# Finding a capacity threshold in four halving rounds, with the gating and picking work laid out in thinner pieces

## The chip, the cores and the metric

The kernel runs on one core of a Trainium2 chip. The metric is the device time of one launch in microseconds, taken as the median of the runs. The core's engines work in parallel, each on its own queue of instructions in program order: TensorE (PE in the profile), VectorE (DVE), ScalarE (ACT), GpSimd (POOL) and SyncE (SP, here only a DMA queue). An instruction that waits holds back everything behind it on its engine.

## The reference, cut to what matters

Eight batches of 2,496 tokens of 256 channels go through a filter in the frequency domain. The 19,968 tokens that come out are gated to eight experts, and each expert keeps the 80 tokens with the largest gate; all other output rows are zero.

```python
X = np.fft.rfft(x, axis=1)                          # x: (8, 2496, 256)
y = np.fft.irfft(X * (filt_r + 1j * filt_i)[None], n=2496, axis=1)
x = y.reshape(8 * 2496, 256)
logits = x @ w_gate                                  # (19968, 8)
expert_idx = np.argmax(logits, axis=1)
probs = softmax(logits); gate_w = probs[arange, expert_idx]
for e in range(8):
    tok_idx = np.where(expert_idx == e)[0]
    if len(tok_idx) > 80:
        tok_idx = tok_idx[np.argpartition(-gate_w[tok_idx], 80)[:80]]
    h = np.maximum(x[tok_idx] @ w1[e], 0.0)          # w1[e]: (256, 1024)
    out[tok_idx] = gate_w[tok_idx, None] * (h @ w2[e])
```

## The kernel before

The length 2,496 is split as 39 x 64, so that the two transforms are matrix products. The last transform is not done for all tokens: the logits come from the half-transformed data, the kept tokens are found, and only rows that may be kept are transformed to the end.

**First phase.** `step(k)` runs for k = 0 to 81, ten steps for each batch. `stage2` of a step is eight matmuls into `pb` (TensorE, L405), one multiplication by the filter into `p` (VectorE, L410) and two combinations into `yt` (GpSimd, L416 and L418). `turn` of the step two back is eight matmuls into `py` (L428), which ScalarE copies out (L450 and L453). `put(k, at, f)` hangs other work on a step: at 0 ahead of `stage2`, at 1 between `stage2` and `turn`, at 2 behind `turn`. The numbers in `put` are written by hand, and they set the order on every engine's queue. Hung on the steps 42 to 72 are:

- `logits_e` (40 matmuls L469, a sum on VectorE) and `logits` of a batch: transposes into `ps` (L481), two copies into `s` on ScalarE (L483), matmuls into `pl` (L490), two copies into `lg` on ScalarE (L495).
- `gating` of one or two batches in six parts: part 0 is a maximum and a difference `sh` on VectorE, then `ex` and `no` on ScalarE (L520, L523); part 1 a DMA; parts 2 and 3 turn `ex` into the `key` on VectorE (L529 to L536, where `key` has the tile of `ex`); part 4 transposes the keys on TensorE into `pk` (L549), copied by ScalarE into `kt`; part 5 finds the eight largest keys of each partition row of a batch, the candidates `cand`.
- `pick`, a generator: each `next` runs it to its next `yield`, one piece. Every partition row belongs to one expert, and 16 rows to each. Its pieces are: the 16 largest candidates of each row, sorted, in `row`, and laid out in `spread`; a matmul that puts all 16 x 16 = 256 of an expert on each of its rows (`pall`, L592) and the count for every one of the 16 sorted values of a row of how many of the 256 are above it; the threshold `tau`, the `kept` candidates and their number `cnt`; offsets through TensorE (`poff`, L632); the compaction into 16 codes (`ccode`); their fields (`fi`, `bval`); two one-hot blocks `bplc` (L687); the list of row indices `idxb` through TensorE (L694). The first pick takes the batches 0 to 4 with a larger share kept, and gives the lists for the gathers; the final pick takes all batches.

The count is the Sign function on ScalarE with its accumulator, one ACTIVATE over 128 x 256 for each of the 16 values:

```python
for k in range(KR):                                   # KR = 16
    nc.scalar.activation(out=pall[:, 256:256 + 16 * KR], in_=pall[:, 0:16 * KR],
                         func=AF.Sign, scale=-1.0, bias=row[:, k:k + 1],
                         accum_out=bal[:, k:k + 1])
    if k % 4 == 3:
        yield
```

`fetch(t)` is a gather on GpSimd's queue (L885): 128 rows of 10 KB, by the list of one batch. The first one stands on step 72, with GpSimd's `yt` operations behind it.

**Second phase.** 41 slots. Slot i transposes four blocks of gathered rows into `pw` (`turn_rows`, L935), which ScalarE copies into `wt` (L936); then `rows_out(i - 1)` multiplies the `wt` of the slot before with kept spectra (eight matmuls into `po`, L948). Five slots make a batch. `aside` gives each slot the work that follows it: logits and gating of the batches 5 to 7, the pieces of the final pick (`last_pick`), loads of spectra and weights. `turn_rows` of a batch's last slot issues the gather of the batch after next.

**Last.** If a count of violations is not zero, a fallback selects again in a slow way; then the two matrix products of the experts run on the gathered rows. One violation is a row that keeps 16 candidates or more (`viol`).

## Time and profile before

| | us |
|---|---|
| median of 3 runs | 510.12 (507.42 to 512.67) |
| profiled execution, its own time | 504.71 |
| its span, first to last instruction | 502.9 |
| TensorE busy in the span | 442.3 (88%) |
| VectorE, ScalarE, GpSimd busy | 174.8, 180.2, 154.0 |

The profiled execution is one more run of the same kernel, 5.4 us under the median of the others, and 1.8 us of its time lie outside the span. A row of the trace gives the start and the duration of an instruction or of a run of equal ones, and in brackets how long its engine had been idle and what it waited for. The steps 0 to 81 lie ahead of about 302 us in the span, the slots of the second phase from about 306 to 397 us.

### The profile page before, as it was taken

What the parts mean: (1) busy time and instruction counts of PE and PEld (TensorE: products, weight loads), DVE (VectorE), ACT (ScalarE), POOL (GpSimd) and SP (SyncE); (2) the same over time, 40 slices, a digit from 0 to 9 for tenths busy, and PEclk for the clock granted to TensorE, in tenths of its full rate; (3) what the DMA queues carried; (4) which work ended last, traced back from release to release, by engine and by line L of the source; (5) the groups of instructions that cost most, each with busy time, mean ns of one, the idle gap of its engine ahead of it and who ended that gap; (6) DMA issues with size and microseconds to landing.
All of it is one profiled execution on the core that took longest, in us unless ns stands there. A gap on an engine that the chain in (4) does not pass through costs nothing. (4 is left out here: it accounts for less than half of the span.)

```text
span 502.9 us, 7871 instructions
## 1 busy us (share of the span) xinstructions
PE 442.3 (88%) x2907; PEld 375.7 (75%) x2907; DVE 174.8 (35%) x344; ACT 180.2 (36%) x452; POOL 154.0 (31%) x218
## 2 busy tenths in 40 slices
PE   4989988889999999879987989985998992799995
PEld 4888766567877878769987988664887882788883
DVE  2555332234434334572858741241430000001100
ACT  1224344453454353751473333538222220001111
POOL 4032212225445443431663780000225003200111
PEclk9999999999999999995997998998999997569999
DMA  6869999998999994696899655359498866929500
GB/s 220 230 197 271 329 354 407 405 361 271 339 287 341 396 398 162 215 314 212 269 371 382 247 186 233 120 202 339 163 376 327 283 224 196 347 72 334 189 15 13
DMA packets 69532, 133.21 MB, mean 265 GB/s; under 512 B 5428, under 2 KB 51892, under 8 KB 67824
## 3 DMA queue, kind: packets, MB, share of 16 engines
q1 hardware_dynamic: 58982, 92.05, 54.6%
q10 hardware_dynamic: 8074, 28.27, 14.2%
q0 software_dynamic: 2432, 12.33, 7.2%
q8 instruction: 25, 0.41, 0.3%
q14 instruction: 19, 0.16, 0.1%
HBM read 81.56 MB, written 51.07 MB: 264 GB/s over the span
## 5 line engine op out<-in xcount | busy, mean ns | idle before, releaser
L410 DVE TENSOR_TENSOR p<-pb,ft 128x1024 f32<-128x1024 f32 x80 | 97.8, 1222 | 96.6 <-PE pb L405 91.0
L416 POOL TENSOR_TENSOR yt<-p 128x256 f32<-128x256 f32 x80 | 60.0, 750 | 176.0 <-PE py L428 114.6
L428 PEld LDWEIGHTS py<-gi,yt 128*128 128x128 f32 x640 | 83.7, 194 | 18.8 <-issue 11.7
L405 PE MATMUL pb<-d_t,t 128*128 128x128 f32 x640 | 88.4, 282 | 7.1 <-ACT t L351 5.8
L428 PE MATMUL py<-gi,yt 128*128 128x136 f32 x640 | 89.9, 284 | 4.6 <-POOL yt L418 4.0
L405 PEld LDWEIGHTS pb<-d_t,t 128*128 128x128 f32 x640 | 80.5, 197 | 10.1 <-ACT t L351 6.5
L349 PE MATMUL pa<-x,wf_t 128*128 128x512 f32 x128 | 60.0, 595 | 0.5 <-ACT t L351 0.4
L418 POOL TENSOR_TENSOR yt<-p 128x256 f32<-128x256 f32 x80 | 58.9, 736 | 0.0
L351 ACT COPY t<-pa 128x512 f32<-128x512 f32 x64 | 36.2, 588 | 51.6 <-PE pa L349 25.7
L948 PE MATMUL po<-yb,wt 128*128 128x256 f32 x160 | 39.9, 394 | 7.7 <-ACT wt L936 7.7
L948 PE MATMUL po<-yk,wt 128*128 128x256 f32 x160 | 37.9, 381 | 2.8 <-ACT wt L936 2.8
L936 ACT COPY wt<-pw 128x512 f32<-128x512 f32 x40 | 23.2, 584 | 47.2 <-PE pw L935 41.8
L948 PEld LDWEIGHTS po<-yb,wt 128*128 128x128 f32 x160 | 29.9, 197 | 11.9 <-ACT wt L936 8.4
L1067 PEld LDWEIGHTS ph<-xs,w 128*128 128x128 f32 x256 | 36.1, 227 | 1.1 <-DVE xs L1063 0.5
L450 ACT COPY ysp<-py 128x512 f32<-128x512 f32 x40 | 23.3, 584 | 37.2 <-PE py L428 24.3
L1067 PE MATMUL ph<-xs,w 128*128 128x80 f32 x256 | 36.1, 311 | 0.3 <-DVE xs L1063 0.3
L349 PEld LDWEIGHTS pa<-x,wf_t 128*128 128x128 f32 x128 | 22.1, 191 | 19.0 <-issue 15.5
L450 ACT COPY yk<-py 128x512 f32<-128x512 f32 x40 | 23.4, 585 | 30.1 <-PE py L428 27.3
L948 PEld LDWEIGHTS po<-yk,wt 128*128 128x128 f32 x160 | 29.1, 191 | 6.4 <-ACT wt L936 3.3
L370 PE MATMUL pn<-wn_t,x 117*128 117x120 f32 x176 | 23.8, 297 | 9.6 <-DMA x<-in_x_dram 8.0
L1081 PE MATMUL po<-w,hT 128*80 128x256 f32 x128 | 31.9, 400 | 0.0
L370 PEld LDWEIGHTS pn<-wn_t,x 117*128 117x128 f32 x176 | 22.8, 212 | 10.1 <-DMA x<-in_x_dram 7.2
(165 smaller groups left out, 384.5 us busy)
## 6 DMA issues: line engine op xcount, KB each, us to landing
out_dram<-zero_t SPq DMA_DIRECT2D x26, 768.0 KB
x<-in_x_dram SPq DMA_DIRECT2D x32, 512.0 KB
d<-t ACTq DMA_DIRECT2D x32, 512.0 KB
w<-in_moe_w_dram SPq DMA_DIRECT2D x16, 1024.0 KB
t<-d SPq DMA_DIRECT2D x30, 512.0 KB
yf<-ysp ACTq DMA_DIRECT2D x20, 512.0 KB
yb<-yf SPq DMA_DIRECT2D x4, 2560.0 KB
x<-in_x_dram SPq DMA_DIRECT2D x25, 156.0 KB
```

The lines of the kernel that those rows point to most:

```text
L349: nc.tensor.matmul(out=ps, lhsT=wf_t, rhs=xt[:, 2 * i:2 * i + 2, :], start=True, stop=True)
L351: nc.scalar.copy(out=t1[:, 2 * i:2 * i + 2, :], in_=ps)
L370: nc.tensor.matmul(out=ps[:, j].rearrange("p h s r -> p (h s r)"), lhsT=xt[0:NP1, j, 128 * cb:128 * cb + 128], rhs=wn_t, start=True, stop= ...
L405: nc.tensor.matmul(out=ps[:, i, cb], rhs=d_t[:, s, :], start=True, stop=True, lhsT=st["t2", b, s // SG][:, s % SG, 128 * cb:128 * cb + 128])
L410: nc.vector.tensor_tensor(out=pt, in0=ps[:].rearrange("p s c r q -> p (s c) r q").unsqueeze(1).to_broadcast(shape), in1=ft[:, u].unsqueeze ...
L416: nc.gpsimd.tensor_tensor(out=yt[:, :, 0, :], in0=pt[:, 0, :, 0, :], in1=pt[:, 1, :, 1, :], op=AL.subtract)
L418: nc.gpsimd.tensor_tensor(out=yt[:, :, 1, :], in0=pt[:, 0, :, 1, :], in1=pt[:, 1, :, 0, :], op=AL.add)
L428: nc.tensor.matmul(out=ps[:, i, 136 * cb:136 * cb + 136], rhs=gi[:, cb, :], lhsT=yt[:, 2 * i + cb].rearrange("p r q -> p (r q)"), start=Tr ...
L450: nc.scalar.copy(out=ys[:, m:m + 2, :].rearrange("p i (k c) -> p i k c", k=NDB), in_=ps[:, :, 0:288].rearrange("p i (k c) -> p i k c", k=N ...
L948: nc.tensor.matmul(po, lhsT=wts[i][:, m, :], rhs=yk[b][g][:, m, :], start=(s == 0), stop=(s == NS - 1))
L1067: nc.tensor.matmul(ph[:, fc // 4, fc % 4, 0:cap], lhsT=w1s[e][:, k, 128 * fc:128 * fc + 128], rhs=xs[:, k, :], start=(k == 0), stop=(k == ...
L1081: nc.tensor.matmul(po[0:cap, :], lhsT=hT[:, fc, :], rhs=w2s[e][:, fc, :], start=(fc == 0), stop=(fc == NFC - 1))
```

## The change

The 256 values on a row are the same as before, and so is the matmul. The 16 counts become four rounds of a halving search over the 16 sorted values: a round counts for one value (the eighth, then by the outcome so far one four, two, one places on), and VectorE works out the next place `at` and picks that value from `row` by a one-hot product with an accumulator. `low`, from which the threshold comes, is then made from the place found. A row may now keep at most 14, not 15, before it counts as a violation, since the search doesn't tell the last place from the end.

The places of the work are changed too. `logits` keep theirs but for batch 4, one step later. `gating(0)`'s six parts stand on the steps 47, 47, 48, 49, 51, 52 (before 47, 48, 48, 48, 49, 50), `gating(2)`'s on 53, 53, 54, 55, 57, 58 (before 50, 51, 51, 51, 52, 53), `gating(4)`'s on 59, 59, 60, 60, 62, 63 (before 54, 55, 55, 56, 57, 58). The pieces of the first pick stand on 64 to 69, 71 to 74 and 76, ahead of `stage2` (before: 59 to 70, behind `turn`), and the first gather on step 76 (before 72). In the second phase the logits and gating of the batches 5 to 7 come up to one slot earlier, the pieces of the final pick one to a slot from slot 9 to 25 (before 8 to 23, three in slot 10), and the gather of batch 5 moves from the transposes of slot 19 to the side work of slot 20.

```diff
--- before.py
+++ after.py
@@ -588,16 +588,37 @@
                 in1=thot[:].unsqueeze(2).to_broadcast([128, 16, KR]), op=AL.mult)
             yield
 
+
             pall = fps.tile([128, 512], F32, name=f"pall_{nm}", tag="f")
             nc.tensor.matmul(pall[:, 0:16 * KR], lhsT=same_f[:],
                              rhs=spread[:].rearrange("p t k -> p (t k)"), start=True, stop=True)
-            bal = tl([128, KR], F32, "bal")
-            for k in range(KR):
+            at = None
+            for i, h in enumerate((8, 4, 2, 1)):
+                if i == 0:
+                    val = row[:, h - 1:h]
+                else:
+                    vrow = tl([128, KR], F32, "vrow")
+                    vt = tl([128, 1], F32, "val")
+                    nc.vector.scalar_tensor_tensor(
+                        out=vrow[:], in0=iota[:, 0:KR], scalar=at[:, 0:1], in1=row[:],
+                        op0=AL.is_equal, op1=AL.mult, accum_out=vt[:, 0:1])
+                    val = vt[:, 0:1]
+                bal = tl([128, 1], F32, "bal")
                 nc.scalar.activation(out=pall[:, 256:256 + 16 * KR], in_=pall[:, 0:16 * KR],
-                                     func=AF.Sign, scale=-1.0, bias=row[:, k:k + 1],
-                                     accum_out=bal[:, k:k + 1])
-                if k % 4 == 3:
-                    yield
+                                     func=AF.Sign, scale=-1.0, bias=val, accum_out=bal[:, 0:1])
+                yield
+
+                nxt = tl([128, 1], F32, f"at{i}")
+                nc.vector.tensor_scalar(out=nxt[:], in0=bal[:], scalar1=16.0 * KR - 2.0 * kc,
+                                        scalar2=float(h), op0=AL.is_ge, op1=AL.mult)
+                if i == 0:
+                    nc.vector.tensor_scalar(out=nxt[:], in0=nxt[:], scalar1=h / 2.0 - 1.0,
+                                            scalar2=None, op0=AL.add)
+                else:
+                    nc.vector.scalar_tensor_tensor(
+                        out=nxt[:], in0=nxt[:], scalar=-h / 2.0 if h > 1 else 0.0, in1=at[:],
+                        op0=AL.add, op1=AL.add)
+                at = nxt
 
 
             if final:
@@ -609,8 +630,8 @@
             nc.vector.tensor_scalar(out=some[:], in0=row[:], scalar1=1e-30, scalar2=None,
                                     op0=AL.is_ge, op1=AL.add, accum_out=npos[:, 0:1])
             low = tl([128, KR], F32, "low")
-            nc.vector.tensor_scalar(out=low[:], in0=bal[:], scalar1=16.0 * KR - 2.0 * kc,
-                                    scalar2=4.0, op0=AL.is_lt, op1=AL.mult)
+            nc.vector.tensor_scalar(out=low[:], in0=iota[:, 0:KR], scalar1=at[:, 0:1],
+                                    scalar2=4.0, op0=AL.is_ge, op1=AL.mult)
             nc.vector.tensor_tensor(out=low[:], in0=low[:], in1=row[:], op=AL.add)
             tau = tl([128, 1], F32, "tau")
             nc.vector.tensor_reduce(out=tau[:], in_=low[:], axis=AX.X, op=AL.min)
@@ -702,7 +723,7 @@
                                     scalar2=None, op0=AL.max)
 
             v0 = 4 * nm
-            nc.vector.tensor_scalar(out=viol[:, v0:v0 + 1], in0=rcnt[:], scalar1=float(KR),
+            nc.vector.tensor_scalar(out=viol[:, v0:v0 + 1], in0=rcnt[:], scalar1=float(KR - 1),
                                     scalar2=None, op0=AL.is_ge)
             vb = tl([128, B], F32, "vb")
             nc.vector.tensor_scalar(out=vb[:, 0:n_b], in0=poff[:, 1, nb0:nb], scalar1=128.0,
@@ -858,22 +879,21 @@
         k = NU * 4 + LATE
         for i in range(3):
             put(k + i, 2, part(logits_e, 0, i))
-        for b in range(4):
-            k = NU * 4 + LATE + 3 + b + b // 2
-            put(k, 1, part(logits, b, 0, 0, b % 2))
-            put(k, 2, part(logits, b, 0, 1, b % 2))
-            if b % 2:
-                for i, at in enumerate((0, 1, 1, 1, 2, 3)):
-                    put(k + 1 + at, 2, part(gating, b - 1, i))
+        for b, at in ((0, 3), (1, 4), (2, 6), (3, 7)):
+            put(k + at, 1, part(logits, b, 0, 0, b % 2))
+            put(k + at, 2, part(logits, b, 0, 1, b % 2))
+        for b0, at0 in ((0, 5), (2, 11)):
+            for i, at in enumerate((0, 0, 1, 2, 4, 5)):
+                put(k + at0 + at, 2, part(gating, b0, i))
 
         k = NU * NA + LATE
         put(k, 2, part(logits_e, 4, 0))
-        put(k + 1, 1, part(logits, 4, 4, 0, 0))
-        put(k + 1, 2, part(logits, 4, 4, 1, 0))
-        for i, at in enumerate((2, 3, 3, 4, 5, 6)):
+        put(k + 2, 1, part(logits, 4, 4, 0, 0))
+        put(k + 2, 2, part(logits, 4, 4, 1, 0))
+        for i, at in enumerate((7, 7, 8, 8, 10, 11)):
             put(k + at, 2, part(gating, 4, i))
-        for at in (7, 8, 9, 10, 11, 12, 13, 14, 15, 16, 17, 18):
-            put(k + at, 2, more_pick)
+        for at in (12, 13, 14, 15, 16, 17, 19, 20, 21, 22, 24):
+            put(k + at, 0, more_pick)
         for i in range(14):
             put(NU * 4 + 4 + 2 * i, 2, part(put_zeros, 1))
 
@@ -892,8 +912,8 @@
             pools["m"] = fctx.enter_context(tc.tile_pool(
                 name="mp", bufs=1, side="right", reuse_waits="tile"))
 
-        put(NU * (B - 1) + LATE - 1, 2, make_room)
-        put(NU * (B - 1) + LATE, 2, part(fetch, 0))
+        put(k + 24, 1, make_room)
+        put(k + 24, 1, part(fetch, 0))
 
         ahead(0)
         chunk()
@@ -934,7 +954,7 @@
                 s = SG * g + m
                 nc.tensor.transpose(ps[:, m, :], gts[t][:, 128 * s:128 * s + 128], ident[:])
             nc.scalar.copy(out=wts[i][:], in_=ps[:])
-            if g == NGR - 1 and t + 2 < B:
+            if g == NGR - 1 and t + 2 < B and t + 2 != NA:
                 fetch(t + 2)
 
         def rows_out(i):
@@ -956,17 +976,18 @@
         fetch(1)
         logits_e(NA, 0)
         logits_e(NA, 1)
-        aside = {0: [part(logits, 5, NA, 0, 0)], 1: [part(logits, 5, NA, 1, 0)],
-                 2: [part(logits, 6, NA, 0, 1)], 3: [part(logits, 6, NA, 1, 1)]}
-        for i, at in enumerate((3, 3, 3, 3, 6, 6)):
+        aside = {}
+        for i, (b, at) in enumerate(((5, 0), (6, 1), (7, 3))):
+            aside.setdefault(at, []).append(part(logits, b, NA, 0, i % 2))
+            aside.setdefault(at + 1, []).append(part(logits, b, NA, 1, i % 2))
+        for i, at in enumerate((2, 2, 2, 3, 4, 5)):
             aside.setdefault(at, []).append(part(gating, 5, i))
-        aside[4] = [part(logits, 7, NA, 0, 0)]
-        aside[5] = [part(logits, 7, NA, 1, 0)]
-        for i, at in enumerate((6, 6, 6, 6, 8, 8)):
+        for i, at in enumerate((5, 5, 6, 6, 7, 8)):
             aside.setdefault(at, []).append(part(gating, 7, i))
 
-        for i in (8, 9, 10, 10, 10, 12, 13, 14, 15, 16, 17, 18, 20, 21, 22, 23):
+        for i in (9, 10, 11, 12, 13, 14, 15, 16, 17, 18, 20, 21, 23, 24, 25):
             aside.setdefault(i, []).append(lambda: next(last_pick, None))
+        aside.setdefault(20, []).append(lambda: fetch(5))
         for i, b in ((1, 3), (6, 4), (15, 5), (20, 6)):
             aside.setdefault(i, []).append(part(spectrum, b))
         aside.setdefault(30, []).append(lambda: load_weights(0))
```

On ScalarE's queue, around the threshold of the final pick: `wt` are the copies that the slots' matmuls wait for, `pall` with `bal` the counts. Before:

```order
L936 COPY wt_3077<-pw_3078 128x512
L596 ACTIVATE pall_3090,bal_3092<-pall_3090,row_3070 128x256 x4
L936 COPY wt_3097<-pw_3098 128x512
L952 COPY yr_3108<-po_3002 128x256
L596 ACTIVATE pall_3090,bal_3092<-pall_3090,row_3070 128x256 x12
L936 COPY wt_3123<-pw_3124 128x512
```

After:

```order
L956 COPY wt_3102<-pw_3103 128x512
L972 COPY yr_3113<-po_3036 128x256
L607 ACTIVATE pall_3116,bal_3118<-pall_3116,row_3095 128x256
L956 COPY wt_3120<-pw_3121 128x512
L607 ACTIVATE pall_3116,bal_3138<-pall_3116,val_3136 128x256
L956 COPY wt_3140<-pw_3141 128x512
L607 ACTIVATE pall_3116,bal_3157<-pall_3116,val_3155 128x256
L956 COPY wt_3160<-pw_3161 128x512
```

The run of twelve counts between two `wt` copies is gone; one count now stands between one `wt` and the next, and it waits for a value that VectorE makes.

On TensorE's queue, around `logits_e` of batch 4 (`pe`) on step 52; `pk` are the transposes of the keys of batches 2 and 3, whose `ex` comes from ScalarE and whose last form from VectorE. Before:

```order
L428 MATMUL py_9_2064<-gi,yt_9_1977 128x136 x4
L405 MATMUL pb_2_2083<-d_t,t_5_1_1947 128x128 x4
L428 MATMUL py_0_2093<-gi,yt_0_2027 128x136 x4
L549 MATMUL pk_2104<-ident,ex_2049 128x128 x4
L469 MATMUL pe_0_2113<-z_1736,e_t 128x16 x20
L405 MATMUL pb_3_2136<-d_t,t_5_1_1947 128x128 x4
L481 MATMUL ps_0_2147<-ident,d_4_2112 20x128 x4
```

After, with ScalarE's queue from the same place in the second piece:

```order
L428 MATMUL py_9_2043<-gi,yt_9_1972 128x136 x4
L549 MATMUL pk_2051<-ident,ex_1910 128x128 x4
L405 MATMUL pb_2_2059<-d_t,t_5_1_1948 128x128 x4
L428 MATMUL py_0_2069<-gi,yt_0_2019 128x136 x4
L469 MATMUL pe_0_2086<-z_1736,e_t 128x16 x20
L405 MATMUL pb_3_2109<-d_t,t_5_1_1948 128x128 x4
L428 MATMUL py_1_2119<-gi,yt_1_2040 128x136 x4
L405 MATMUL pb_4_2136<-d_t,t_5_2_1950 128x128 x4
L481 MATMUL ps_0_2147<-ident,d_4_2085 20x128 x4
```

```order
L520 ACTIVATE ex_2131<-sh_2129 128x512
L523 ACTIVATE no_2133,firsts<-sh_2129 128x512
L483 COPY s_4_2146<-ps_0_2147 20x512
L483 COPY s_4_2146<-ps_1_2153 20x512
L450 COPY ysp_1_2164<-py_2_2159 128x512
```

The `pk` ahead of `pe` is now that of batches 0 and 1, one step earlier and made from an `ex` four steps old; the `pk` of batches 2 and 3 moved behind step 57, and the copies of batch 4's `s` now stand behind `ex` and `no` of batches 2 and 3.

On VectorE's queue, around the threshold of the first pick; `p` are the products of the steps, which GpSimd and then TensorE wait for. Before:

```order
L586 TENSOR_TENSOR spread_2326<-row_2321,thot 128x256
L410 TENSOR_TENSOR p_0_2333<-pb_0_2328,ft 128x1024
L410 TENSOR_TENSOR p_1_2361<-pb_1_2356,ft 128x1024
L410 TENSOR_TENSOR p_2_2383<-pb_2_2378,ft 128x1024
L410 TENSOR_TENSOR p_3_2408<-pb_3_2403,ft 128x1024
L410 TENSOR_TENSOR p_4_2430<-pb_4_2425,ft 128x1024
L609 TENSOR_SCALAR some_2445,npos_2446<-row_2321 128x16
L612 TENSOR_SCALAR low_2448<-bal_2350 128x16
```

After:

```order
L586 TENSOR_TENSOR spread_2404<-row_2399,thot 128x256
L410 TENSOR_TENSOR p_4_2411<-pb_4_2406,ft 128x1024
L410 TENSOR_TENSOR p_5_2436<-pb_5_2431,ft 128x1024
L612 TENSOR_SCALAR at_0_2449<-bal_2429 128x1
L615 TENSOR_SCALAR at_0_2449<-at_0_2449 128x1
L602 SCALAR_TENSOR_TENSOR vrow_2452,val_2453<-iota,at_0_2449,row_2399 128x16
L410 TENSOR_TENSOR p_6_2462<-pb_6_2457,ft 128x1024
L612 TENSOR_SCALAR at_0_2478<-bal_2455 128x1
L618 SCALAR_TENSOR_TENSOR at_0_2478<-at_0_2478,at_0_2449 128x1
L602 SCALAR_TENSOR_TENSOR vrow_2481,val_2482<-iota,at_0_2478,row_2399 128x16
```

Between two `p` there now stand three small operations of a round, and the first of them waits for a count on ScalarE of the step before.

## Rows read from the trace of the kernel before

**Rows 1.** TensorE's waits: line, waited for, total us, times, longest us.

```profile
PE po L948 <- ACT wt L936: 10.5, 5, 5.3
...
PE pk L549 <- DVE ex L536: 3.1, 1, 3.1
...
PE pl L490 <- ACT s L483: 1.4, 1, 1.4
...
PE pall L592 <- DVE some L609: 0.7, 1, 0.7
```

**Rows 2.** Timeline of plain steps: start, us, engine, line, tiles, [idle <- released by].

```profile
283.10 1.09 PE L428 MATMUL py<-gi,yt 128*128 128x136 f32 x8
283.36 1.22 DVE L410 TENSOR_TENSOR p<-pb,ft 128x1024 f32<-128x1024 f32 x1 [0.58 <-PE pb L405]
...
285.41 0.73 POOL L418 TENSOR_TENSOR yt<-p 128x256 f32<-128x256 f32 x1
...
286.74 1.09 PE L428 MATMUL py<-gi,yt 128*128 128x136 f32 x8
```

**Rows 3.** Windows: length, busy us of PE, PEld, DVE, ACT, POOL, granted clock, DMA.

```profile
225.00:240.00 15.00, 14.58 (x84) 13.25 (x85) 4.62 (x11) 3.32 (x8) 2.81 (x4) 0.66 0.72 242
260.00:275.00 15.00, 11.32 (x75) 11.01 (x76) 9.95 (x31) 7.48 (x27) 5.18 (x8) 0.77 1.07 385
293.00:294.00 1.00, 1.00 (x12) 1.00 (x11) 0.63 (x1) 0.67 (x2) 0.23 (x1) 1.00 0.18 72
300.00:315.00 15.00, 14.39 (x97) 12.07 (x97) 1.32 (x2) 5.48 (x11) 1.60 (x2) 0.89 0.57 241
345.00:355.00 10.00, 4.90 (x16) 4.01 (x17) 1.26 (x9) 5.83 (x19) 0.00 (x0) 0.66 0.61 213
```

**Rows 4.** Timeline, TensorE: the first step beside the counts of the first pick.

```profile
253.94 1.09 PE L428 MATMUL py<-gi,yt 128*128 128x136 f32 x8
```

**Rows 5.** Lines: the counts, both picks: busy us, mean ns | idle before.

```profile
L596 ACT ACTIVATE pall<-pall,row 128x256 f32<-128x256 f32 x32 | 14.4, 450 | 4.0 <-PE pall L592 2.6 <-ACT z L453 0.6
...
L596 ACT ACTIVATION_READ_ACCUMULATOR pall<-pall,row 128x1 f32 x32 | 6.2, 195 | 0.0
```

**Rows 6.** Timeline: the first gather and the step behind it.

```profile
287.71 1.03 POOL L885 DMA_INDIRECT gt<-rows_tbl,idxb  x1 [1.56 <-ACT z L453]
...
290.22 1.19 PE L428 MATMUL py<-gi,yt 128*128 128x136 f32 x8 [1.49 <-POOL yt L418]
```

**Rows 7.** Windows, as in group 3, around VectorE's gating and pick pieces.

```profile
235.96:246.48 10.52, 10.52 (x83) 9.70 (x80) 7.52 (x17) 5.42 (x15) 4.52 (x7) 0.91 0.82 282
251.23:252.38 1.15, 1.15 (x13) 1.15 (x12) 1.05 (x6) 0.39 (x2) 0.92 (x2) 1.00 0.93 187
...
267.95:277.95 10.00, 9.04 (x62) 8.85 (x61) 9.69 (x22) 2.02 (x6) 6.10 (x7) 0.79 1.07 381
```

**Rows 8.** Timeline: equal operations with GpSimd busy and idle, and GpSimd's beside `bplc`.

```profile
270.99 1.48 DVE L666 TENSOR_SCALAR fi<-ci 128x16 int32<-128x16 int32 x4
...
274.69 1.57 POOL L416 TENSOR_TENSOR yt<-p 128x256 f32<-128x256 f32 x1 [2.25 <-DVE p L410]
...
358.04 0.41 DVE L666 TENSOR_SCALAR fi<-ci 128x16 int32<-128x16 int32 x4
```

**Rows 9.** Timeline of the second phase, TensorE and ScalarE.

```profile
333.60 1.99 PE L948 MATMUL po<-yk,wt 128*128 128x256 f32 x8 [1.74 <-ACT wt L936]
...
350.10 3.78 PE L948 MATMUL po<-yb,wt 128*128 128x256 f32 x8 [5.35 <-ACT wt L936]
...
367.85 1.89 PE L948 MATMUL po<-yb,wt 128*128 128x256 f32 x8
...
370.02 1.89 PE L948 MATMUL po<-yb,wt 128*128 128x256 f32 x8
...
385.89 0.58 ACT L936 COPY wt<-pw 128x512 f32<-128x512 f32 x1 [4.99 <-issue]
386.53 1.99 PE L948 MATMUL po<-yb,wt 128*128 128x256 f32 x8 [1.98 <-ACT wt L936]
```

## The prediction

> **What bounds the kernel now.** TensorE is busy for 88% of the span, so what can be won are its waits and the stretches in which its clock is low. I read first the list of TensorE's waits [rows 1]: in the stretch that the change touches they are the matmuls of a slot waiting for ScalarE's `wt` (10.5 us in five waits), `pk` waiting for the keys (3.1), `pl` waiting for the copies of `s` (1.4) and `pall` (0.7). Then the timeline of undisturbed steps [rows 2]: from `py` at 283.10 to the `py` at 286.74 lie two steps, 1.82 us each; VectorE idles 0.58 in a step, and the second `yt` of the step is done at 285.41 + 0.73 = 286.14, 0.60 ahead of the `py` at 286.74. So a step takes 0.58 us of extra VectorE work for nothing, and a single backlog of 0.60 more. Third the windows [rows 3], for the granted clock: 0.66 in the 15 us behind the wait for `pk`, 0.77 in the first pick, 0.66 around the longest wait of the second phase; between 2.4 and 1.2 GHz, 0.66 over 15 us is (1 - 0.66) x 15 = 5.1 us of full-speed work lost.
>
> What the first phase loses before: `pl` 1.4 and `pk` 3.1 [rows 1], the clock behind it 5.1 [rows 3]. The first pick: from the `py` at 253.94 [rows 4] to the one at 283.10 [rows 2] lie 11 steps, 29.2 us where 11 x 1.82 = 20.0 and some 0.8 of the pick's own matmuls were due, so 8.4 (its share in the clock is within it: 0.77 over 15 us is 3.5). The cause is ScalarE: 16 counts of 0.450 + 0.195 = 0.645 us are 10.3 us [rows 5], put in blocks of four between the copies of the steps, and the threshold can't start before the last. The first gather: `py` at 290.22 instead of 286.74 + 1.82, 1.7 [rows 2, 6]. Sum 1.4 + 3.1 + 5.1 + 8.4 + 1.7 = 19.7 us.
>
> **What the first phase loses after.** *The counts.* Four instead of 16 of 0.645 us, one in a step, beside copies of 0.78 in 1.82: ScalarE is no longer the limit, and the 8.4 us go as far as nothing else is late. *The keys.* `pk` now has two steps between its last input and itself, so the 3.1 us go. *`pl`.* The wait of 1.4 stays for the first batches (the same copies stand behind the same `ex`), and on step 54 the order makes a second one of the kind, with `ex` and `no` of the batches 2 and 3 ahead of the `s` of batch 4: another 1.4. *The clock behind `logits_e`.* The 40 small matmuls stay. Their other occurrence, without a wait ahead of it, has 0.89 over 15 us [rows 3], 1.7 lost; with the wait it was 5.1. The new place has no wait of 3.1, but the one of 1.4 shortly behind. I take 3.1, nearer the undisturbed row, ends 1.7 and 4.5.
>
> *VectorE's load.* Part 5 of two batches and the parts 0, 2 and most of 3 of batch 4 took, in the stretch from 235.96, 7.52 busy less three `p` of 1.22, 3.9 us [rows 2, 7]. After the change they stand on three adjacent steps, 58 to 60: 3.9 less 3 x 0.58 less 0.60 is 1.6 late. The first piece of the pick is 1.05 [rows 7], behind another part 5, 0.2. From offsets to the second `bplc` the pieces are 9.69 - 3 x 1.22 = 6.0 [rows 7], now on the four steps 71 to 74 ahead of each `p`: 6.0 - 4 x 0.58 - 0.60 = 3.1 late. Together 4.9, ends 2.5 (the parts that lie in `at` 2 have a further step's cover) and 7.
>
> *The rounds.* Three small operations on VectorE in a round, 11 in all, are each some 0.2 us alone and fit in the 0.58. But beside GpSimd the same kind of work is not always small: four `fi` took 1.48 us with GpSimd busy and 0.41 with it idle, and a `yt` beside `bplc` 1.57 where 0.73 is usual [rows 2, 8]. That is 0.27 an operation, so at most 11 x 0.27 = 2.9 and at least nothing; GpSimd is busy 1.46 of 1.82, so I take 2.0. *The gather.* Between nothing more than its 1.03 less the 0.60 and the 1.7 of before [rows 6]: 1.0. What is hidden: the count's own round trip, because a whole step lies between a count and the operation that reads it. If it were not hidden, `p` would wait behind it, and with it `yt` and `py`, four times about 0.6.
>
> Sum after: 2.8 + 3.1 + 4.9 + 2.0 + 1.0 = 13.8; gain 19.7 - 13.8 = 5.9 us, ends 1 and 10.
>
> The Trainium skill, page "SBUF — State Buffer", section "Who interferes with whom", speaks against this part: a VectorE operation with two inputs in SBUF and a GpSimd operation that reads SBUF exclude each other, and the later one waits for the whole of the other. The `fi` rows have one input, which by the page contend only in a mode with two ports; the pair of 1.48 and 0.41 agrees with an exclusion and doesn't say which form of it. By the rule the six two-input operations among the 11 would each wait for up to a `yt`; if every one waited for a whole one, 6 x 0.73 = 4.4 us stood in place of my 2.0 and the time would be 497, which is inside the range.
>
> **The second phase.** A slot is 370.02 - 367.85 = 2.17 us [rows 9], all TensorE's. Of the waits for `wt`, the longest is 5.35 [rows 9]: the twelve counts in a row (12 x 0.645 = 7.7 us) stand ahead of one `wt`. With one count of 0.645 behind a `wt` of 0.58 ScalarE needs 1.23 of 2.17. So 5.35 goes, with the 0.38 of the four counts, with the 0.7 of `pall`, and with the clock behind it: 0.66 over 10 us is 3.4 [rows 3], of which 2.0 fall on matmuls (3.78 instead of 1.89 for the eight at 350.10 [rows 9]). The 1.74 at 333.60 [rows 9] comes from `ex` and `no` of batch 7 waiting for `sh`, behind parts of batch 5 on VectorE; they are now on slots of their own: gone. A further 1.06 at the gating of batch 5 keeps its neighbours and stays. Gain 5.35 + 0.38 + 0.7 + 2.0 + 1.74 = 10.2. The gather of batch 5 starts a slot later: it has five slots, 10.8 us, and one alone took from 287.71 to shortly after 293, some 5.7 [rows 3, 6]; but a load of 2.6 MB starts beside it. Stall between 0 and 3, taken 0.5. The fifth wait, 1.98 at 386.53, comes from 4.99 us in which ScalarE waited for nothing that the trace shows [rows 9]; its place may shift with 24 fewer instructions ahead, 0 to 2 us of gain, and since nothing names it, I take 0. Net 9.7.
>
> **Sum.** 5.9 + 9.7 = 15.6 us. The profiled execution (504.71 us) would become 489.1; the median of the runs is 5.4 above it, and the same difference gives 510.12 - 15.6 = **494.5 us**.
>
> **The rivals.** *A. The first phase gives nothing.* VectorE's pieces bunch up behind each other and behind GpSimd, 7 + 2.9 us of lateness, and the clock falls again behind `logits_e` (4.5) and the gather (1.7): 2.8 + 4.5 + 7 + 2.9 + 1.7 = 18.9 against 19.7. With the gather of batch 5 late by 3 in the second phase the gain is 0.8 + 7.2 = 8.0: 502 us; with a further new wait of two or three us there, 505. For it: the load really is put on adjacent steps. Against it: the same gating parts before, at full clock, cost next to nothing. *B. More is won.* No clock loss beyond 1.7, half of the VectorE lateness, no exclusion, gap at 386 gone: 2.8 + 1.7 + 2.5 + 0 + 0.4 = 7.4, gain 12.3 + 10.2 + 2.0 = 24.5: 485.5. *C. Slower.* The new idles of one to two us on the steps 54, 58 to 60, 64 and 71 to 74 make TensorE's clock fall and keep it at 1.2 GHz. A step at that level is about twice 1.82, which hides VectorE's lateness but costs 1.82 for each: from 54 to 74, 20 steps are 36.4, less some 7 hidden, and the kernel is at 523. The point from which it decides is some eleven steps at the low level. For it: the windows of 0.66 and 0.77 [rows 3], each behind waits of about 3. Against it: behind the wait of 1.49 at 290.22 [rows 6] the clock was 1.00 [rows 3]. *D. The counts don't go.* If each round's count came so late that the `wt` behind it is late too, by 2 us in each of four slots, or the new limit of 14 sent the kernel into the fallback. Against the first: VectorE has only small work in these slots; against the second: 80 kept in 16 rows are five in a row on average, far from 15. A time of 503 for the first; the fallback would be slower than everything here.
>
> **How the numbers follow.** About 1% (5 us) is what a measurement of this kernel tells from no change. Chances: the forecast 0.57, A 0.2, B 0.13, C 0.05, D 0.05 (fallback under 0.01 of it). Range: from 486, close to B, to 504, which takes in most of A and the first half of D; C lies outside. Faster by over 1% means under 505.0: the forecast, B, most of A and of D, 0.86; within 1% 0.09; slower 0.05.
>
> **What would show it.** In the profile after: 8 counts instead of 32, TensorE's waits for `wt` down from 10.5 to about 3, no wait for `pk`; the window after `logits_e` of batch 4 at a clock of about 0.8; the 11 steps of the pick at 1.82 to 2.2 us each. A VectorE that is busy without a gap from step 71 to 74, with TensorE waiting for `yt`, would show my term for its load right. The prediction is wrong if the rounds' operations wait for ScalarE (the count isn't hidden), if the clock is low for more than five steps, or if slot 25 waits for its rows.

## The result and the profile after

The changed kernel takes 491.33 us in the median (489.58 to 492.45, 4 runs), the kernel before 508.77 in the same series (505.65 to 512.67): a ratio of 0.965, interval 0.957 to 0.973. Medians here and below are of all runs of a kernel, while the ratios leave out its slow ones, those over 1.5% above the fastest of their kernel. The forecast was 494.5, with a range from 486 to 504. The sum came out, in part by luck: the late gather cost far more than its term, a wait that was taken to stay went, and the reason given for the gain in the first pick holds for a part of it only.

TensorE's waits after (line, what it waited for, total, times, longest) answer to [rows 1]:

```profile
PE py L428 <- POOL yt L418: 6.3, 8, 2.4
...
PE pw L955 <- DMA gt<-rows_tbl,idxb: 3.9, 1, 3.9
...
PE pl L490 <- ACT s L483: 2.2, 2, 1.4
...
PE po L968 <- ACT wt L956: 1.3, 2, 1.1
```

The wait for `pk` is gone, the waits for `wt` fell from 10.5 to 1.3 us; `yt` is waited for more, and a wait for gathered rows is new. Two waits of before that the prediction didn't list, though they lie in the stretch that changes, are these; `poff` is no longer waited for:

```profile
PE py L428 <- POOL yt L418: 4.0, 5, 1.5
...
PE poff L632 <- DVE cnt L627: 2.8, 1, 2.8
```

The windows after, with the columns of [rows 3]:

```profile
210.00:225.00 15.00, 13.61 (x102) 11.49 (x101) 7.70 (x10) 9.07 (x21) 6.56 (x10) 0.89 0.98 336
225.00:240.00 15.00, 14.23 (x97) 13.33 (x96) 8.80 (x16) 4.45 (x13) 4.90 (x7) 0.77 0.92 311
255.00:270.00 15.00, 14.08 (x120) 13.63 (x119) 13.51 (x31) 6.54 (x21) 9.86 (x15) 1.00 1.06 384
270.00:285.00 15.00, 10.47 (x86) 9.73 (x85) 14.27 (x34) 3.95 (x12) 8.69 (x11) 1.00 0.89 325
366.00:374.00 8.00, 3.56 (x12) 2.92 (x12) 0.72 (x5) 0.58 (x1) 6.11 (x7) 0.64 0.99 361
```

Behind `logits_e` the clock is 0.77 instead of 0.66, in the first pick 1.00 instead of 0.77. VectorE (the third busy time) is full from 270 to 285, 14.27 of 15. The counts, both picks (busy, mean ns):

```profile
L607 ACT ACTIVATE pall<-pall,val 128x256 f32<-128x256 f32 x6 | 2.7, 451 | 1.8 <-DVE vrow L602 1.8
...
L607 ACT ACTIVATE pall<-pall,row 128x256 f32<-128x256 f32 x2 | 0.9, 448 | 0.4 <-PE pall L593 0.3
```

Eight in place of 32, at the duration of [rows 5]. The first operation of a round that reads a count, on VectorE:

```profile
L612 DVE TENSOR_SCALAR at<-bal 128x1 f32<-128x1 f32 x8 | 1.2, 146 | 8.3 <-ACT pall L607 8.3
```

The 8.3 us of waiting for a count are four waits, all in the final pick, where VectorE has time; in the first pick it waits for none. The timeline of the changed kernel, first the rounds and VectorE's late stretch, then slot 25:

```profile
263.63 0.14 DVE L612 TENSOR_SCALAR at<-bal 128x1 f32<-128x1 f32 x1
...
264.00 0.62 DVE L602 SCALAR_TENSOR_TENSOR vrow<-iota,at,row 128x16 f32<-128x16 f32 x1
...
264.04 1.09 PE L428 MATMUL py<-gi,yt 128*128 128x136 f32 x8
...
265.86 1.09 PE L428 MATMUL py<-gi,yt 128*128 128x136 f32 x8
...
275.16 1.19 PE L428 MATMUL py<-gi,yt 128*128 128x136 f32 x8 [1.47 <-POOL yt L418]
...
284.20 1.19 PE L428 MATMUL py<-gi,yt 128*128 128x136 f32 x8 [2.42 <-POOL yt L418]
...
335.68 0.23 DVE L602 SCALAR_TENSOR_TENSOR vrow<-iota,at,row 128x16 f32<-128x16 f32 x1
...
358.13 1.87 POOL L905 DMA_INDIRECT gt<-rows_tbl,idxb  x1 [15.37 <-PE pw L955]
...
370.76 1.09 PE L955 MATMUL pw<-ident,gt 128*128 128x128 f32 x4 [3.89 <-DMA gt<-rows_tbl,idxb]
371.64 3.60 PE L968 MATMUL po<-yk,wt 128*128 128x256 f32 x8
```

Beside the rounds the steps run at 1.82 us (264.04 to 265.86): `vrow` takes 0.62 us beside GpSimd and 0.23 in the final pick, and TensorE doesn't feel it. At 284.20 it waits 2.42 for a `yt` that is late behind VectorE's pieces. In slot 25 it waits 3.89 for the gather of batch 5, and the eight matmuls behind take 3.60 instead of 1.89.

### The profile page after: what moved, and what is told of

It reads as the page before. It is cut to its first block, busy times and chain, and to the rows that moved or that the text cites. A ratio compares the mean times of both kernels' runs of the same rounds, so it can differ in the third digit from the quotient of the medians.

```text
span 490.7 us, 7854 instructions
## 1 busy us (share of the span) xinstructions
PE 440.4 (90%) x2907; PEld 374.8 (76%) x2907; DVE 180.3 (37%) x372; ACT 167.9 (34%) x404; POOL 154.4 (31%) x218
## 3 DMA queue, kind: packets, MB, share of 16 engines
q1 hardware_dynamic: 58982, 92.05, 56.5%
## 5 line engine op out<-in xcount | busy, mean ns | idle before, releaser
L349 PE MATMUL pa<-x,wf_t 128*128 128x512 f32 x128 | 61.5, 609 | 0.3 <-ACT t L351 0.3
L968 PE MATMUL po<-yk,wt 128*128 128x256 f32 x160 | 39.6, 393 | 1.3 <-ACT wt L956 1.3
L968 PE MATMUL po<-yb,wt 128*128 128x256 f32 x160 | 37.8, 379 | 0.0
L968 PEld LDWEIGHTS po<-yb,wt 128*128 128x128 f32 x160 | 28.8, 190 | 3.1
```

The lines of the kernel that those rows point to most:

```text
L349: nc.tensor.matmul(out=ps, lhsT=wf_t, rhs=xt[:, 2 * i:2 * i + 2, :], start=True, stop=True)
L968: nc.tensor.matmul(po, lhsT=wts[i][:, m, :], rhs=yk[b][g][:, m, :], start=(s == 0), stop=(s == NS - 1))
```

## The experiments

The theory: ScalarE's counts bound the first pick and the longest wait of the second phase, and the keys' wait with its clock loss is the rest. The rival: the places are worth more than the rounds. For each run I give its median, and three stretches from the starts in its trace (`py` issued by step 44, by step 60, the last `py`, and `px`, the first work of the experts), which hold the same work in every order: logits and gating; first pick and gather; second phase. Before, they take 56.5, 49.1 and 129.5 us, after 53.4, 47.4 and 121.3. Each stretch is read from one trace. Kernels of one series are compared with each other, since the medians of before differ by series (504.1 to 508.8). The changed kernel itself ran in none of the series below; the kernel with its load two slots later (490.51), in which the load started at the same place, stands for it in the first.

**Rounds alone, places of before.** The change of `pick` without one of `put` or `aside`.

```diff
-            for k in range(KR):
...
+            for i, h in enumerate((8, 4, 2, 1)):
...
-                if k % 4 == 3:
-                    yield
...
+                yield
```

Expected: 

> The kernel before with the four halving rounds and the limit of 14, all places as before. My theory (ScalarE's 16 counts bound the first pick and held one wt copy in the second phase, and the places are worth less than the rounds): the first pick's 8.4 us fall to about 1.5, the three rounds that stand together in slot 10 take some 4 us in place of 7.7 and hold the wt copy by 1 to 2 instead of 5.35, with no clock loss behind it; the wait for pk (3.1) and the clock behind it (5.1) stay, as does the 1.74. Gain about 7 + 6 = 13 us, about 496. Rival (the places carry the gain, the counts were only late because of where they stood): 503 or more.

501.86 against 506.06, ratio 0.988 (0.983 to 0.994). Stretches 58.1, 51.4, 121.6: the second phase gains 7.9, near the 8.2 of the changed kernel; the first phase gains nothing, and is 4.0 longer in this pair of traces. The wait for `wt` behind the counts is 1.43 instead of 5.35, as was expected. The theory's half on the second phase holds; on the first pick it falls.

**Places alone, 16 counts.** The changed kernel with the counting loop of before and its limit.

```diff
-            for i, h in enumerate((8, 4, 2, 1)):
...
+            for k in range(KR):
...
+                if k % 4 == 3:
+                    yield
```

Expected: 

> The changed kernel with the 16 counts of before, in four blocks of four at the new places. My theory: four counts of 0.645 and the copies of 0.78 make 3.4 us on ScalarE where a step has 1.82, so 4 x 1.5 = 6 us are lost in the first pick; in the second phase 2.58 + 0.58 = 3.2 against 2.17 lose 1.0 in each of four slots; the 3.1 of pk and part of the clock are gained, the late gather of batch 5 stays. About 502 to 503. Rival (the places carry the gain): within 2 us of the changed kernel, about 493.

495.23 against 506.06, ratio 0.977 (0.968 to 0.987). Stretches 51.0, 49.2, 124.8. The time lies between the two and nearer the rival, though not within its 2 us: of the 15.6 us between 506.06 and 490.51 the places carry 10.8, some two thirds. The four counts in a step cost much less than was expected: in the first pick `py` stands 0.77 and 1.18 us where the copies on ScalarE are late (6 expected), and in the second phase the four slots of the counts wait 1.3 us for `wt` (4 expected).

**First phase as before, all else changed.**

```diff
-        for at in (12, 13, 14, 15, 16, 17, 19, 20, 21, 22, 24):
-            put(k + at, 0, more_pick)
+        for at in (7, 8, 9, 10, 11, 12, 13, 14, 15, 16, 17, 18):
+            put(k + at, 2, more_pick)
```

(logits, gating and first gather alike.) Expected: 

> The changed kernel with the places of the first phase as before (logits, gating, first pick, first gather), rounds in both picks and the new places in the second phase. My theory: the first pick is freed of the counts all the same; the wait for pk of 3.1 and the clock behind it (5.1) are back, but VectorE's pieces are spread better over the steps: 3 us slower than the changed kernel, about 494. Rival (the first phase's places give nothing or cost): equal to or faster than the changed kernel, 488 to 491.

502.40 against 506.06, and against 490.51 of the next kernel in the same series: the first phase's places are worth 12 us in the medians, 5.9 in the one pair of traces. Where the 8.4 us of the first pick went is seen in its timeline, the same places as before but with rounds:

```profile
265.67 0.17 PE L653 MATMUL poff<-cnt,before 128*128 128x5 bf16 x1 [1.74 <-DVE cnt L648]
...
275.78 1.19 PE L428 MATMUL py<-gi,yt 128*128 128x136 f32 x8 [2.42 <-POOL yt L418]
...
290.57 1.19 PE L428 MATMUL py<-gi,yt 128*128 128x136 f32 x8 [3.06 <-POOL yt L418]
```

In the kernel before, the counts did hold the threshold: VectorE stood 4.57 us for the last of them, and `poff` 2.80 for VectorE.

```profile
265.54 0.17 DVE L612 TENSOR_SCALAR low<-bal 128x16 f32<-128x16 f32 x1 [4.57 <-ACT pall L596]
```

Without the 16 counts `poff` still waits, 1.74: it stands one step behind the threshold that it needs. The clock is 1.00 from 260 to 290, so the 3.5 us of low clock are gone. But TensorE now waits for `yt` behind VectorE's pieces (2.42) and behind the first gather on step 72 (3.06), where it had waited 0.96 and 1.49 before. So the gain is given back in the same stretch (48.8 against 49.1): TensorE's waits there are 9.6 us, where before they were 7.4 with 3.4 of low clock. That the low clock had hidden the load of VectorE is how I read these numbers; no run separates it.

**The load two slots later.**

```diff
-        for i, b in ((1, 3), (6, 4), (15, 5), (20, 6)):
+        for i, b in ((1, 3), (6, 4), (15, 5), (22, 6)):
...
-        for i in (3, 7, 12, 16, 22, 26):
+        for i in (3, 7, 12, 16, 26, 28):
```

Expected: 

> The changed kernel with the 2.6 MB load of the spectrum of batch 6 moved from slot 20 to slot 22, and two of the zero-filling writes from slots 22 and 26 to 26 and 28. Theory 1 (the gather of batch 5 is late because 3.4 MB of other transfers run beside it): the wait of 3.9 us of slot 25 falls under 1, and the half clock behind it (eight matmuls in 3.60 instead of 1.89) goes: 5 to 6 us faster than the changed kernel, about 486. Theory 2 (the gather is late because it starts a slot later, and its descriptors took 1.87 us on GpSimd instead of 0.95): the wait stays above 3, about 491.

490.51; slot 25 still waits 4.8. It decides nothing: SyncE's queue had nothing to wait for in between, and the load was issued 0.88 us ahead of the gather as in the changed kernel.

**The load behind slot 25's store.**

```diff
-        for i, b in ((1, 3), (6, 4), (15, 5), (20, 6)):
+        for i, b in ((1, 3), (6, 4), (15, 5), (25, 6)):
```

Expected: 

> The changed kernel with the load of the spectrum of batch 6 put on slot 25, where it stands on SyncE's queue behind a store that waits for slot 25's result (on slot 22 it started as early as on slot 20, since nothing ahead of it on that queue waited). Theory 1 (the gather of batch 5 shares the transfers with this load of 2.6 MB): the load leaves, the gather lands some 6 us after its issue, the wait of 3.9 to 4.8 us of slot 25 falls under 1 and the half clock behind it goes, 5 us faster than the changed kernel, about 486. Theory 2 (four slots, 8.8 us from issue to use, are too few even alone): the wait stays above 2, about 490. Either way slot 31 may wait for the load if it comes too late.

486.57 (483.39 to 488.39), 4 to 5 us under the two kernels of its series that differ from the changed one elsewhere (490.33 and 491.50). Second phase 115.3 instead of 121.3. Its timeline in slot 25 and at the load's use:

```profile
363.90 0.63 PE L955 MATMUL pw<-ident,gt 128*128 128x128 f32 x4
...
378.48 1.75 PE L968 MATMUL po<-yb,wt 128*128 128x256 f32 x7 [0.96 <-DMA yb<-yf]
```

No wait for the gather, and slot 31 waits 0.96 for the load. So it was the 2.6 MB beside it: the first of the two theories. The margin is small: alone, the gather landed 8.3 us after its issue, not 6, and slot 25 needed it 8.7 after.

**The list and the gather a slot earlier.**

```diff
-        for i in (9, 10, 11, 12, 13, 14, 15, 16, 17, 18, 20, 21, 23, 24, 25):
+        for i in (9, 10, 11, 12, 13, 14, 15, 16, 17, 18, 19, 21, 23, 24, 25):
...
-        aside.setdefault(20, []).append(lambda: fetch(5))
+        aside.setdefault(19, []).append(lambda: fetch(5))
```

Expected: 

> The changed kernel with the list of row indices made one slot earlier (19) and the gather of batch 5 issued there; the 2.6 MB load stays on slot 20. The gather starts about 2.2 us earlier and ahead of the load: if it is only its start that is late, the wait of 3.9 to 4.8 falls to between 0 and 2 and the clock behind it comes back: 3 to 5 us faster, about 487. If the transfers of the load push it anyway, the wait stays above 2.

491.50, and slot 25 waits 4.9: starting 1.7 us ahead of the load (356.70 and 358.43) doesn't help, the gather landed 15.7 us after its issue. In the kernel before, the same gather was issued 4.5 us ahead of the load (368.29 and 372.76), and slot 25 didn't wait; how large a lead is enough, no run was made to show.

**Gating and logits as before, first pick at its new places.**

```diff
-            for i, at in enumerate((0, 0, 1, 2, 4, 5)):
-                put(k + at0 + at, 2, part(gating, b0, i))
...
+                for i, at in enumerate((0, 1, 1, 1, 2, 3)):
+                    put(k + 1 + at, 2, part(gating, b - 1, i))
```

(logits and `gating(4)` alike.) Expected: 

> The changed kernel with logits and gating of the first phase at the places of before, the first pick and the first gather at the new places. Theory 1 (the wait for the keys ahead of the 40 small matmuls and the low clock from there on are most of what the first phase's places give): the wait for pk of 3.1 is back, the stretch from step 50 to step 60 takes 34 to 35.5 us instead of 27.4 to 29.7, and the kernel takes about 498. Theory 2 (the first pick's new places, with the threshold and the offsets apart, give it): within 2 us of the changed kernel, 490 to 493.

497.62, 6 to 7 over two kernels of its series that keep the new gating places (490.33 and 491.50); stretches 57.9, 47.9, 121.2, so the difference is in the first. Theory 1 holds. The wait and the slow small matmuls are back, right behind each other:

```profile
225.69 1.11 PE L549 MATMUL pk<-ident,ex 128*128 128x128 f32 x4 [3.10 <-DVE ex L536]
226.59 8.55 PE L469 MATMUL pe<-z,e_t 128*128 128x16 f32 x40
```

**The kernel before, `pk` behind the small matmuls.**

```diff
-                for i, at in enumerate((0, 1, 1, 1, 2, 3)):
+                for i, at in enumerate((0, 1, 1, 1, 2, 3) if b < 3 else (0, 1, 1, 1, 3, 4)):
```

Expected: 

> The kernel before with one thing moved: the transposes pk of the keys of batches 2 and 3, and the candidates behind them, one step later, behind the 40 small matmuls of logits_e (counts and all other places as before). Theory 1 (the wait of pk ahead of the small matmuls, and the low clock that they then run at, is the larger part of what the first phase's places give): the wait of 3.1 goes, the small matmuls take 4.5 to 6 us instead of 6.9 to 8.5, and the kernel is 4 to 8 us faster than before: ratio 0.985 to 0.992. Theory 2 (the wait moves to another place, such as the copies of s of batch 4 or the step's p, since VectorE has the same work at the same places): within 2 us of before.

501.93 against 508.20, ratio 0.989 (0.986 to 0.992): one place moved by one step is worth what the rounds alone were. There is no wait for `pk`, the granted clock from 225 to 240 is 0.77 instead of 0.66, and the small matmuls take less time:

```profile
222.84 6.05 PE L469 MATMUL pe<-z,e_t 128*128 128x16 f32 x40
```

**Logits a step later.**

```diff
-        for b, at in ((0, 3), (1, 4), (2, 6), (3, 7)):
+        for b, at in ((0, 3), (1, 4), (2, 7), (3, 8)):
...
-        put(k + 2, 1, part(logits, 4, 4, 0, 0))
+        put(k + 3, 1, part(logits, 4, 4, 0, 0))
```

Expected: 

> The changed kernel with the logits of batches 2, 3 and 4 one step later, so that the copies of s no longer stand directly behind ex and no of the pair of batches before. If the waits of pl (1.4 and 0.8) come from that order on ScalarE, both go, with the clock of 0.89 in the 15 us around the first: 2 to 4 us faster than the changed kernel, 487 to 489. If they come from the transposes or from VectorE, no change.

490.33 (487.93 to 495.22). Both waits of `pl` are gone, and the first stretch takes 49.6 against 51.0 to 53.4 of the kernels in the order of the changed one. The clock from 210 to 225 is 1.00, but so it is in the run with the load on slot 25, where the first of the waits still stands, so the 0.89 isn't shown to come from it. In the total nothing is resolved, and the 487 to 489 were not reached. It shows one thing more: with no wait anywhere ahead of them, the small matmuls (4.92) are still followed by matmuls at half speed:

```profile
224.32 4.92 PE L469 MATMUL pe<-z,e_t 128*128 128x16 f32 x40
229.08 2.06 PE L405 MATMUL pb<-d_t,t 128*128 128x128 f32 x8
```

**Both: load on slot 25, logits later.**

```diff
-        for b, at in ((0, 3), (1, 4), (2, 6), (3, 7)):
+        for b, at in ((0, 3), (1, 4), (2, 7), (3, 8)):
...
-        for i, b in ((1, 3), (6, 4), (15, 5), (20, 6)):
+        for i, b in ((1, 3), (6, 4), (15, 5), (25, 6)):
```

Expected: 

> The changed kernel with the load of the spectrum of batch 6 on slot 25 and the logits of batches 2 to 4 one step later. If the two gains are separate (5 us and 2.6 us in their stretches): about 484. If the second was noise, as its total of 490.3 may say: 486.5.

485.54 (483.27 to 488.12, 6 runs), ratio 0.957 (0.952 to 0.962): the lowest median of the study, 1 us under that of the load alone, which these runs, of two series, can't separate.

**The last pieces of the first pick further apart, on top of both.**

```diff
-        for at in (12, 13, 14, 15, 16, 17, 19, 20, 21, 22, 24):
+        for at in (12, 13, 14, 15, 16, 17, 19, 20, 22, 23, 25):
```

Expected: 

> As the run with both, and the last five pieces of the first pick on the steps 71, 72, 74, 75, 77 instead of 71 to 74 and 76, the first gather on 77. If VectorE's lateness there is a matter of spacing, each further free step takes 0.58 us: 0.6 to 1.2 us faster than the run with both. If it is a matter of the amount of work (10.6 us on the steps 69 to 77 against 0.58 us of room in each), no change. Slower if the first gather, a step later, is waited for.

488.24, ratio 0.961 (0.956 to 0.967): no gain, and 2.7 us more than the run with both, in the medians. TensorE's waits for `yt` are 5.2 instead of 5.6, the largest 1.6 instead of 2.4: the lateness is spread, and hardly less. That speaks for the amount of work, not the spacing. What it costs is the third thing that was expected, the first gather that comes too late; it is slot 0 that waits for it:

```profile
301.05 1.08 PE L955 MATMUL pw<-ident,gt 128*128 128x128 f32 x4 [2.90 <-DMA gt<-rows_tbl,idxb]
```

The load of batch 3's spectrum on slot 1 is issued 0.6 us behind this gather (288.68 and 289.30), and slot 0, ready 9.5 us behind it, still waits; in the run with both the load comes 2.4 us behind it (287.17 and 289.61), and slot 0 doesn't wait. That looks like the late gather of slot 25 once more, at another slot.

**Counts again, with the load on slot 25.** The places-only kernel, 16 counts and their limit, with the load's place.

```diff
-        for i, b in ((1, 3), (6, 4), (15, 5), (20, 6)):
+        for i, b in ((1, 3), (6, 4), (15, 5), (25, 6)):
```

Expected: 

> The new places, the load on slot 25, and the 16 counts instead of the rounds: what the rounds are worth when the gather doesn't cover anything. By the stretches of the earlier runs (0 to 2 us in the first phase, 3.5 in the second) it takes 3.5 to 5.5 us more than the same with rounds, 490 to 492. If the rounds are worth nothing but their place on ScalarE, 487.

492.50 (489.66 to 493.50), 7 us over the run with both in the same series; the logits' places, which differ too, are in these 7. The pair of earlier runs (495.23 and 490.51) has 4.7. So I put the rounds at 4 to 6 us at the new places, an estimate from these two pairs. It waits for `wt` eight times, 4.7 us in all, but only 1.3 of that in the four slots of the counts, less than half of the 3.5 expected; the run with both waits 3.4 at the other slots.

## Why the prediction was right, step by step

**Sum.** 15.6 us forecast, 17.4 measured in the medians, 12.3 in the one pair of profiled executions: the profiled one of before was among its quick ones (first stretch 56.5; the three other kernels in that order took 57.8 to 58.1). By the stretches of that pair the first phase gives 4.7 where 5.9 were forecast, the second 8.2 where 9.7 were.

**The keys and the clock behind `logits_e`.** Right in mechanism, small in size. Forecast 3.1 + 5.1 + 1.4 less 2.8 + 3.1, that is 3.7 us; the first stretch is shorter by 3 to 7, and going back to the old places costs 6 to 7 in the median. The step that was mis-sized is the clock of before: 0.66 in the profiled execution, but 0.54 over the same 15 us in the run with the old gating, and 8.55 us for the small matmuls against 6.91 in the trace that I read. That the clock falls behind the 40 small matmuls without any wait was right: 0.77 over 15 us in the trace of the changed kernel, 3.4 us against my 3.1.

**The first pick.** "The cause is ScalarE" is the step that failed here. The counts did hold the threshold (4.57 us of VectorE's time before), but the 8.4 us don't go with them: rounds at the old places take 48.8 and 51.4 where before it was 49.1, and 16 counts at the new places take 49.2 where rounds take 47.4. Once the counts are gone, the chain from threshold to `poff` one step apart, VectorE's load and the gather's place bind the same stretch. The net of this part, 10.1 less 7.9 = 2.2 us, was near the 1.6 of the traces by luck, by terms that replaced each other. VectorE's lateness with the rounds and the gather was put at 7.9; the waits for `yt` went from 4.0 to 6.3. The rounds' own 2.0 didn't appear between the steps: VectorE took 2.05 us for each, 0.23 over TensorE's 1.82, which the backlog of 0.60 took up. It came in the threshold piece, 2.6 us from 269.77 to 272.42. The steps of the pieces behind it are not the 1.82 to 2.2 us that were forecast: from 271.46 to 284.20 four of them take 12.7 us.

**The exclusion.** `vrow`, two inputs in SBUF, took 0.62 us beside GpSimd and 0.23 without; the first ended at 264.62, the `yt` that ran beside it at 264.58. This agrees with the Trainium skill, page "SBUF — State Buffer", section "Who interferes with whom". The `at` operations with two inputs took 0.16; each began just before a `yt`, so they show nothing of an exclusion. What the rounds cost the step was 0.91 us of VectorE's time, 0.23 of it not covered.

**The second phase.** With the rounds alone the stretch is 7.9 us shorter, and the waits for `wt` fall from 10.5 to 6.3; with the pieces spread too they are 1.3 (about 3 were forecast). Spreading seems to add nothing (121.3 against 121.6), but only because the late gather takes it: with the load moved, the stretch takes 115.3 and 118.3 in two traces, 3 to 6 us less than with the rounds alone. The step that failed is the gather of batch 5: "it has five slots, 10.8 us ... taken 0.5". It is issued behind slot 20's rows, at 358.13, and slot 25 stands ready at 366.87: four slots, 8.7 us. It got 12.6, since the load of 2.6 MB ran beside it; wait 3.9 and half clock 1.7 make 5.6 in place of 0.5, and outside the 0 to 3 that were allowed. Without it the kernel is at 486.6. The sum of the phase came near all the same, since a wait that was taken to stay, 1.98 us at 386.53 before, isn't in the changed kernel; why, no run shows.

**Rivals.** A's late gather came true, at more than its price of 3; B's time was reached once the load was moved. C didn't come: behind the waits of 1.47 and 2.42 the clock stayed at 1.00 in the changed kernel. It did fall elsewhere: 0.89 over 15 us around the wait of 1.39 for `pl`, 0.77 behind the small matmuls, and beside the 3.89 of slot 25. And in the run with the later logits it was 0.83 from 280 to 290, behind the same pieces; each time it came back within a few steps. D didn't come: the longest wait for `wt` is 1.1, and no fallback is in the trace. Of the prediction's own signs of being wrong, one came: slot 25 waits for its rows. The gain stood all the same.

## What to carry to other kernels

What an engine holds up doesn't come back whole when its work goes: ask what else stands between the same two points, and whether a slow TensorE hides it. Here a wait of 3.1 us directly ahead of many small matmuls cost 2 to 5 us more in clock than the same matmuls without it; move the waiting instruction behind them before anything else is made faster. For a transfer that is used at a fixed slot, count the slots from its issue in the order, and look at what the other queues start in that time: here each late gather had a load of 2.6 MB issued within 2 us of it.

## What the runs showed of the hardware

In one series the times of the kernel before go with its mean granted clock: 501.56 us at 0.946, 508.86 at 0.930, and the nine others in between. In another series they do so less: 504.47 us came at 0.936, 509.79 at 0.943. The changed kernel's four runs lie within 3 us at 0.948 to 0.955.

The instruction of a gather took 1.87 us on GpSimd where it began beside VectorE's `eplc` (two inputs in SBUF; in the changed kernel and most of the experiments), and 0.94 to 1.03 elsewhere. The prediction has no term for it; why a gather's instruction should wait for it, no run here shows. By itself it cost nothing seen: with the load on slot 25 it took 1.87 too, and slot 25 didn't wait.

A gather of 128 rows landed 6.2 us after its issue with a load of 2.6 MB issued 2.4 us behind it (the first of the changed kernel) and 8.3 with none near it (batch 5, load on slot 25). With a load issued within 2 us of it, ahead or behind, it took 12.4 (the first, last pieces further apart), 12.6 (batch 5, changed kernel) and 15.7 (batch 5, earlier list).
